# Two tiles' scores issued together in the first layer of a four-layer attention kernel, and its first chunk projected in blocks

## The chip, the cores and the metric

The kernel runs on one core of a Trainium2 chip. The metric is the time of the whole program on the device, in microseconds (us); the median of several executions counts. Engines are named as in the profile: PE (matmuls) and PEld (its weight loads), ACT (the scalar engine), DVE (the vector engine), POOL (GpSimd) and SP (the sync engine, which here issues most DMAs).

## The reference

Four layers in a row: A, B, A, B. Each normalises x, attends, projects and adds to x. A and B have weights of their own. The sequence is S = 2048, D = 640, 32 heads of 20. A attends in a causal window of 256 positions, B attends to all 2048 positions.

```python
def _A_ref(x, wqkv, wo):
    B, S, D = x.shape
    H = 32; Dh = D // H; W = 256
    qkv = (x @ wqkv).reshape(B, S, 3, H, Dh)          # shortened
    q, k, v = ...
    scores = jnp.einsum("bhqd,bhkd->bhqk", q, k) * (Dh ** -0.5)
    idx = jnp.arange(S)
    mask = (idx[:, None] - idx[None, :] >= 0) & (idx[:, None] - idx[None, :] < W)
    scores = jnp.where(mask[None, None], scores, -1e9)
    p = _softmax(scores, axis=-1)
    o = jnp.einsum("bhqk,bhkd->bhqd", p, v)
    return o.transpose(0, 2, 1, 3).reshape(B, S, D) @ wo
# _B_ref: the same without the mask
x = x + _A_ref(_layernorm(x), A_wqkv, A_wo)
x = x + _B_ref(_layernorm(x), B_wqkv, B_wo)
x = x + _A_ref(_layernorm(x), A_wqkv, A_wo)
x = x + _B_ref(_layernorm(x), B_wqkv, B_wo)
```

All tensors are bf16.

## The kernel before

**Units, sets and tiles.** The queries are worked on in four chunks of 512 (C = 512, c = 0 to 3), the heads in eight groups of four (g = 0 to 7). Layers are l = 0 to 3. A `Unit(l, c, g)` is the attention of one group for one chunk. It consists of sets: the scores of one head, one bank of PSUM, up to 512 columns. A windowed unit (layers 0 and 2) has 12 sets; those of the first chunk are partly narrower (512, 384 and 256 columns). Of the second layer's first chunk the units are cut into parts of four key blocks (16 sets each); 24 such early units are woven in among the first layer's later units, from (l, c, g) = (0, 1, 7) on. `index` numbers the units in their order: unit 16 is the first of the early ones, number 47 is (0, 3, 7), the last windowed unit of the first layer.

Sets are taken from the units in order into tiles. As long as units are narrow (the first layer and the early units), a tile has three sets when its number t is even and two when t is odd. Even tiles use banks 0 to 2 of PSUM, odd ones banks 3 and 4. Banks 5 and 6 serve the background work, bank 7 (`op`) sums the values.

**The main loop** (L1389 to L1559) does one tile per turn. It writes a fixed order of instructions:

1. the scores on PE (L1436: `lhsT` keys, `rhs` queries, 32 rows of the array each, up to four heads side by side);
2. one exp on ACT (L1462), or several where the widths differ, from PSUM into a tile `pt`;
3. background work (`background`, L1373), before the values while `state["early"]` holds and behind them otherwise;
4. the values: groups of four sets, at least three tiles old where the unit is windowed (L1495: 21 columns of the array for each head, summed in `op`);
5. the masks of the tile before: POOL (L1535) and DVE (L1546) zero parts of `pt`.

**Background work** is a list of tasks (`todo`) of Python generators, in the order of `need - lead`: `need` is the number of the unit that wants the result. `pump` lets tasks run for a credit per tile: 1.2 us up to unit 16, at most 1.0 after it. `require` runs tasks at once until something is ready. Tasks are the normalisation (`t_ln`), value projections (`t_v`), query and key projections in blocks of 128 rows (`t_block`), the output projection (`t_out`), and the tails of finished units, which divide by the sums. All of their matmuls go through `by_columns` (L311, shown as L315): four strips of 32 output columns side by side. Results leave PSUM through `evac`: on ACT (L345) up to unit 16, on DVE (L348) after it. `keep_clock` adds matmuls without a use (`masks,ident`) where a tile has little background.

**Queries and keys.** `t_block` casts a block of 128 rows to `st`, and POOL stores it to DRAM (`q_d`, `k_d`, L566). `load_unit` later loads a group's rows head by head from there into a slot of `qa` (4 slots) and of `ka` (18 slots), with eight DMAs on SP (L802, L803): 20 rows for each head at partitions 0, 32, 64 and 96. `load_ahead` starts the loads as soon as the blocks are ready and a slot is free. The first chunk of the first layer is different: `t_qk_first` projects each of the eight groups by itself, with weights padded from 20 to 32 columns a head (`get_w`: a memset on POOL and a copy on DVE), straight into `qa` and `ka`, without DRAM:

```python
        wt = take_w(0, g)
        q = qa_free.popleft()
        yield from project(wt, xnT[l, c], lambda: q[:])
        wt = take_w(1, g)
        k = ka_free.popleft()
        yield from project(wt, xnT[l, c], lambda: k[:])
```

`project` is five steps of four matmuls of 512 columns, and then `evac`.

**The beginning.** SP loads x's first chunk in two halves, then the first layer's query, key and value weights, the other chunks of x, and the second layer's value weights (L128 to L138). `first_ln` (L1254) normalises the first chunk; 14 matmuls without a use come first on PE (`warm(14)`, L1266), more stand between the transposes (L1284). `other_constants` zeroes `op` and builds the constants of the tails. `t_zeros` (L1232) zeroes `wop`, `kts` and `qts` by DMAs from zeroed `ka` slots, and loads the output weights (`load_wop`).

Of the kernel before, what the change touches and what calls it, by code (L numbers as in the profile page):

```python
# [18 lines left out]
P = 128  # L19
S = 2048  # L20
D = 640
# [24 lines left out]
KEEP = 30  # L46
HALF = True
# [10 lines left out]
def kernel(  # L58
# [77 lines left out]
    for c in range(1, NC):  # L136
        nc.sync.dma_start(out=x_sb[:, 4 * c : 4 * c + 4, :], in_=xin[:, 4 * c : 4 * c + 4, :])
    nc.sync.dma_start(out=wv_sb[1][:], in_=wq_view[1][:, :, 2 * D : 3 * D])  # L138
# [32 lines left out]

    nc.vector.memset(ka_all[:, G:KA, :], 0.0)

    def other_constants():
        nc.vector.memset(op, 0.0)
        nc.vector.tensor_copy(
            out=sel4[:], in_=ident[:].rearrange("p (j m) -> p j m", j=4)[:, :, DH]
        )

        nc.gpsimd.memset(spread8[:], 0.0)  # L180
        nc.gpsimd.memset(rts[:], 0.0)
        sp32 = rzp.tile([64, 2, 16], BF16, name="sp32", tag="sp32")
        sp16 = rzp.tile([64, 16], BF16, name="sp16", tag="sp16")
        for u in range(2):
            r = slice(32 * u, 32 * u + 32)
            nc.vector.tensor_copy(
                out=sp32[r], in_=ident[r, r].rearrange("p (n r) -> p n r", n=2)
            )
            nc.vector.tensor_tensor(
                out=sp16[r], in0=sp32[r, 0, :], in1=sp32[r, 1, :], op=ALU.add  # L190
            )
            nc.vector.tensor_copy(
                out=spread8[r, u].rearrange("p q (j m) -> p (q j) m", m=32),
                in_=sp16[r].unsqueeze(2).to_broadcast((32, 16, 32)),
            )
# [22 lines left out]
    def push(name, gen, need, left):  # L218
        lead = 0
        if type(name) is tuple and need <= first_use(1, NC - 1, 0):  # L220
# [3 lines left out]
            if name[0] in ("k", "q"):  # L224
                lead = 7 if name[1] == 1 and name[-1] == 0 else 2

            if name[0] == "stats" or name[:2] == ("ln", 0):
                lead = 5
# [82 lines left out]
    def by_columns(out_, lhsT, rhs, start, stop):  # L311

        for j in range(4):
# [39 lines left out]
    padded = [0]  # L353

    def get_w(n, i):

        a = padded[0] % 8 * P
        padded[0] += 1
        t = wqk[:, :, a : a + P]
        tv = t.rearrange("p c (j m) -> p c j m", j=4)  # L360
        nc.gpsimd.memset(tv[:, :, :, DH:32], 0.0)
# [18 lines left out]
    def block_w(l, n, b):  # L380

        a = n * D + b * P
# [13 lines left out]
    def project(wt, xt, dst):  # L396
# [6 lines left out]
        evac(dst(), pq)  # L403
# [17 lines left out]
    def t_ln(l, c):  # L421
# [3 lines left out]
        users[l, c] = 9 if (l, c) == (0, 0) else (11, 12, 11, 11)[l]  # L425
# [50 lines left out]
    def t_v(l, c, halves):  # L476
# [9 lines left out]
        for i in range(4):  # L486
            if windowed:
# [46 lines left out]
    ka_free = deque(kas)  # L534
    qa_free = deque(qas)

    def t_qk_first(l, c, g):
# [13 lines left out]
        if g == G - 1:  # L551
            nc.sync.dma_start(out=wqk[:], in_=wq_view[1][:, :, 0 : 8 * P])
            nc.sync.dma_start(out=wqk_rest, in_=wq_view[1][:, :, 8 * P : 2 * D])
            ready.add("weights")

    def t_block(l, n, c, b):
# [5 lines left out]
        wt = block_w(l, n, b)  # L562
        yield from project(wt, xnT[l, c], staged)
        rows = slice(b * P, (b + 1) * P)
        dst = k_d[l][rows, c * C : (c + 1) * C] if n else q_d[l][c, rows, :]
        nc.gpsimd.dma_start(out=dst, in_=staging.pop())  # L566
        used(l, c)
        ready.add(("qk"[n], l, c, b))
# [68 lines left out]
    def push_layer(l, c):  # L637
# [18 lines left out]
        for g in range(G):  # L656
            for n in (0, 1):
                worder[l, n].append((n, g))
            push(("qk", l, c, g), t_qk_first(l, c, g), need[g], 2.2)
            if g == 0:  # L660
                push(("v", l, c), t_v(l, c, (0, 1)), need[0], 5.6)
# [118 lines left out]
    small_units = deque(u for u in units if u.windowed and (u.l, u.c) != (0, 0))  # L780
# [45 lines left out]
    def unit_needs(u):  # L826
        l, c, g = u.l, u.c, u.g
        if (l, c) == (0, 0):
            return [("qk", l, c, g)]
# [27 lines left out]
    def start_unit(u):  # L857
        for n in unit_needs(u):
            require(n)
        if (u.l, u.c) != (0, 0):  # L860
# [371 lines left out]
    def t_zeros():  # L1232

        z = ka_all[:, G : G + 4, :].rearrange("p a b -> p (a b)")
        yield ("wait", 4)
# [6 lines left out]
        load_wop(0, False)  # L1242
        for t in (*kts, *qts):
# [10 lines left out]
    def first_ln():  # L1254

        users[0, 0] = 9
# [9 lines left out]
        warm(14)  # L1266
# [23 lines left out]
        for i in range(4):  # L1290
# [8 lines left out]
            if i > 0:  # L1299
                trs.append(scale(i - 1))  # L1300
                warm((0, 3, 2)[i - 1])
        nc.vector.tensor_copy(out=xt[:, :, 0:P], in_=trs[0])
        trs.append(scale(3))
        warm(3)
        nc.vector.tensor_copy(out=xt[:, :, P : 2 * P], in_=trs[1])
        for n in (1, 0):
            wtiles[n, 0] = get_w(n, 0)
        nc.vector.tensor_copy(out=xt[:, :, 2 * P : 3 * P], in_=trs[2])
        nc.scalar.copy(out=xt[:, :, 3 * P : 4 * P], in_=trs[3])
        mvs.pop((0, 0))  # L1310
# [3 lines left out]
    with tc.manual_schedule():  # L1314
# [4 lines left out]
        other_constants()  # L1319
# [60 lines left out]

        wide_pt = 0
        started = set()
        pts = deque()
        masked = None
# [3 lines left out]
        closed = -2  # L1388
        while ended is None or t < ended + 8:  # L1389
            t += 1  # L1390
            state["tick"] += 1
            n_b = 0
            if flow:
# [76 lines left out]
                if state["early"]:  # L1470
                    background(t, n_b)
# [4 lines left out]
            for n in range(2 if n_b == 0 or t > closed + 1 else 0):  # L1476
                u = pts[0][3][0] if pts else None
                size = 4
                if u is not None:
                    size -= sum(kc == pts[0][3][4][0][0] for kc, _ in u.aside)  # L1480
                if len(pts) < size or pts[size - 1][0] > t - n - (3 if u.windowed else 2):
                    break
                group = [pts.popleft() for _ in range(size)]
                subs, end = group[0][3][4], group[-1][3][7]
                if end and u.aside and pts and not side_ready(u) and group[-1][0] > t - 5:
                    pts.extendleft(reversed(group))
                    break
                first, last = group[0][3][5:7]
                if first and u.windowed:
                    require(("v", u.l, u.c, 0))  # L1490
                    require(("v", u.l, u.c, 1))
                for m, (kc, q0, qn, col) in enumerate(subs):
                    for _, pg, i, b in group:
                        j = b[1]
                        nc.tensor.matmul(  # L1495
                            op[32 * j : 32 * j + VW, q0 * P : (q0 + qn) * P],
                            lhsT=u.v(kc, j), rhs=pg[:, i, col * P : (col + qn) * P],
                            start=(first and m == 0), stop=not u.windowed or (last and m == len(subs) - 1),
                            skip_group_check=True,
                        )  # L1500
                if u.aside:
                    if end:
                        side_done(u)
                    else:
                        side_values(u, 3)
                if end:
                    pv_emitted(u)
                    finish_unit(u)
                    closed = t
                    break  # L1510

            if n_b and not freely():
                side_work(False, PRE_1)
            if n_b and not state["early"]:
                background(t, n_b)
            if n_b:
                side_work(False)
                columns = sum((4 - b[3]) * P for b in cur)
                state["lag"] = max(state["lag"] - columns / 1200 - 0.05, 0.0)

            if t > 0 and masked is not None:
                cur_, pt_ = masked
                i = 0
                while i < len(cur_):
                    m, b0 = cur_[i][2:4]
                    k = i
                    while k < len(cur_) and cur_[k][2] == m:
                        k += 1
                    split = m is not None
                    for b in ((3,), (1, 2), (0,))[m] if split else ():  # L1530
                        if b < b0:
                            continue
                        later = (m, b) in ((1, 1), (0, 3))
                        v = pt_[:, i:k, b * P : (b + 1) * P]
                        nc.gpsimd.affine_select(  # L1535
                            out=v, in_=v, compare_op=ALU.is_gt if later else ALU.is_ge, fill=0.0,
                            base=0, pattern=[[0, k - i], [-1 if later else 1, P]],
                            channel_multiplier=1 if later else -1,
                        )
                    if split and m != 1:  # L1540
                        cols = slice(max(b0, 0) * P, 2 * P) if m == 0 else slice(2 * P, C)
                        mv_ = masks[:, m, cols].unsqueeze(1).to_broadcast(
                            (P, k - i, cols.stop - cols.start)
                        )
                        state["lag"] += 0.45
                        nc.vector.tensor_tensor(  # L1546
                            out=pt_[:, i:k, cols], in0=pt_[:, i:k, cols], in1=mv_, op=ALU.mult
                        )
                    elif m is not None and not split:
                        cols = slice(max(b0, m == 1) * P, 3 * P if m == 1 else C)  # L1550
                        mv_ = masks[:, m, cols].unsqueeze(1).to_broadcast(
                            (P, k - i, cols.stop - cols.start)
                        )
                        state["lag"] += 0.45
                        nc.vector.tensor_tensor(
                            out=pt_[:, i:k, cols], in0=pt_[:, i:k, cols], in1=mv_, op=ALU.mult
                        )
                    i = k
            masked = (cur, pt) if n_b else None  # L1559
# [35 lines left out]
```

## Time and profile before

| what | us |
|---|---|
| median of 3 runs (lowest to highest) | 2161.81 (2161.41 to 2163.21) |
| the profiled execution's own time | 2161.74 |
| its span, first to last instruction | 2160.0 |
| PE busy | 1926.8 (89%) |
| ACT busy | 2088.0 (97%) |
| DVE busy | 1467.3 (68%) |
| POOL busy | 361.5 (17%) |
| exps (L1462), 1641 of them | 2054.0 |

The span is one execution, seen by the hardware profiler; 1.7 us of its own time lie outside of it. Busy time of PE counts a matmul from its start to its modelled end, so matmuls that follow each other closely overlap, and a busy PE need not be at its peak. A row of a timeline gives the start and the length of merged instructions, engine, line, operation, what is written from what, shapes (rows of the array by columns, then elements), the count, and in brackets how long the engine stood idle before it and for what.

### The profile page before, as it was taken

The numbers are of one execution on the slowest core, as the hardware profiler recorded it, in microseconds if no ns is written. First come the engines' busy times: TensorE is split into PE (matmuls) and PEld (weight loads), VectorE is DVE, ScalarE is ACT, GpSimd is POOL, SyncE is SP. The second block draws the span as 40 slices with busy tenths as digits, with TensorE's granted clock in tenths as the row PEclk, the third lists the DMA queues.
The fourth block names the chain that finished last, engine by engine and source line by source line (L and its number), as shares of the span: only waits on it lengthen the run. The fifth ranks groups of instructions, "written<-read, shape, count | busy, mean of one in ns | idle before, by whom it ended". The sixth has DMA issues, their size and how long they took to land. (4 is left out here: it accounts for less than half of the span.)

```text
span 2160.0 us, 73146 instructions
## 1 busy us (share of the span) xinstructions
PE 1926.8 (89%) x31790; PEld 757.8 (35%) x31791; DVE 1467.3 (68%) x2613; ACT 2088.0 (97%) x1717; POOL 361.5 (17%) x805
## 2 busy tenths in 40 slices
PE   8899999988889898888988989888898988888898
PEld 4444443433333333333333433342332222222222
DVE  6556665426666776776767743773588888987886
ACT  7889899999999999999999999999999999999997
POOL 6543434000022002400033001500000000000000
PEclk9999999999999999999999999999999999999999
DMA  6212122222110222111120122111111111111100
GB/s 204 65 54 75 54 62 69 67 63 59 55 42 27 63 53 69 38 31 48 50 83 27 33 60 75 33 45 52 54 57 44 36 36 42 32 33 39 44 27 17
DMA packets 81440, 114.33 MB, mean 53 GB/s; under 512 B 20990, under 2 KB 63070, under 8 KB 81118
## 3 DMA queue, kind: packets, MB, share of 16 engines
q1 hardware_dynamic: 71502, 81.06, 14.2%
q0 software_dynamic: 9616, 28.59, 3.8%
q8 instruction: 249, 4.08, 0.8%
q14 instruction: 73, 0.60, 0.1%
HBM read 76.58 MB, written 27.79 MB: 48 GB/s over the span
## 5 line engine op out<-in xcount | busy, mean ns | idle before, releaser
L1462 ACT ACTIVATE pt<-ps 128x1536 bf16<-128x1536 f32 (+2 forms) x1641 | 2054.0, 1417 | 38.5 <-PE ps L1436 28.9
L1436 PE MATMUL ps<-qt,kt 32*128 32x512 bf16 x3913 | 543.6, 384 | 62.8 <-ACT pt L1462 55.7
L315 PE MATMUL ps<-masks,ident 128*32 128x512 bf16 x5684 | 507.6, 384 | 94.7 <-ACT pt L1462 49.1
L1495 PE MATMUL ps<-pt,vt 128*21 128x512 bf16 x3784 | 377.1, 386 | 0.3 <-ACT pt L1462 0.2
L1436 PEld LDWEIGHTS <-kt 32*128 32x128 bf16 x3913 | 155.5, 91 | 460.1 <-issue 440.8
L315 PEld LDWEIGHTS <-ident 128*32 128x32 bf16 x5684 | 182.2, 94 | 283.4 <-issue 256.7
L1535 POOL TENSOR_SCALAR_AFFINE_SELECT pt<-pt 128x256 bf16<-128x256 bf16 (+2 forms) x508 | 219.0, 453 | 198.6 <-ACT pt L1462 185.8
L348 DVE CAST st<-ps 128x512 bf16<-128x512 f32 x134 | 92.6, 691 | 144.8 <-PE ps L315 144.5
L1495 PEld LDWEIGHTS <-vt 128*21 128x21 bf16 x3784 | 93.7, 89 | 254.2 <-issue 250.5
L315 PE MATMUL ps<-wop,on 128*32 128x320 bf16 x3712 | 160.7, 300 | 4.5 <-DVE x_sb L598 2.6
L1007 DVE TENSOR_SCALAR spare<-ps 128x512 int32<-128x512 f32 x200 | 137.2, 686 | 27.8 <-PE ps L989 24.1
L315 PEld LDWEIGHTS <-on 128*32 128x32 bf16 x5760 | 122.8, 95 | 62.3 <-issue 28.4
L1546 DVE TENSOR_TENSOR pt<-pt,masks 128x256 bf16<-128x256 bf16 (+3 forms) x270 | 117.0, 449 | 39.5 <-ACT pt L1462 37.6
L1436 PE MATMUL ps<-qa,ka 32*128 32x384 bf16 (+2 forms) x1408 | 118.5, 275 | 22.9 <-ACT pt L1462 19.6
L1203 DVE TENSOR_TENSOR on<-on,ps 128x512 bf16<-128x512 bf16 x128 | 86.4, 684 | 59.0 <-PE ps L315 56.9
L598 DVE TENSOR_TENSOR x_sb<-x_sb,ps 128x320 bf16<-128x320 bf16 x120 | 58.3, 486 | 100.3 <-PE ps L315 99.5
L315 PE MATMUL ps<-wv,xnT 128*32 128x320 bf16 x2560 | 117.1, 303 | 9.5 <-DVE on L1203 3.0
L315 PE MATMUL ps<-xnT,spare 128*32 128x512 bf16 x1720 | 118.0, 381 | 5.5 <-DVE on L1203 1.8
L315 PE MATMUL ps<-xnT,wqk 128*32 128x512 bf16 x1600 | 107.7, 381 | 4.6 <-DVE rts L1182 1.3
L1007 DVE TENSOR_SCALAR raw_o<-ps 128x512 int32<-128x512 f32 x112 | 76.8, 686 | 47.6 <-PE ps L1436 46.7
L900 DVE CAST on<-ps 128x512 bf16<-128x512 f32 x112 | 76.7, 685 | 35.5 <-PE ps L1495 28.5
L566 POOL DMA_DIRECT2D k_d<-st x75 | 41.6, 555 | 270.9 <-DVE st L348 248.0
(103 smaller groups left out, 1731.6 us busy)
## 6 DMA issues: line engine op xcount, KB each, us to landing
vt<-v_d SPq DMA_DIRECT2D x48, 336.0 KB
kt<-k_d SPq DMA_DIRECT2D x192, 80.0 KB
k_d<-st POOLq DMA_DIRECT2D x75, 128.0 KB, 2.2
q_d<-st POOLq DMA_DIRECT2D x75, 128.0 KB, 2.1
qt<-q_d SPq DMA_DIRECT2D x384, 20.0 KB
v_d<-vs POOLq DMA_DIRECT2D x16, 336.0 KB, 3.0
qa<-q_d SPq DMA_DIRECT2D x224, 20.0 KB
ka<-k_d SPq DMA_DIRECT2D x224, 20.0 KB
```

Of the source, the lines that this page charges most:

```text
L315: nc.tensor.matmul(out_[r], lhsT=lhsT[:, r], rhs=rhs, start=start, stop=stop)
L348: nc.vector.tensor_copy(out=out_, in_=in_)
L566: nc.gpsimd.dma_start(out=dst, in_=staging.pop())
L598: nc.vector.tensor_tensor(out=xv, in0=had, in1=yp, op=ALU.add)
L900: nc.vector.tensor_copy(out=oT, in_=op)
L1007: nc.vector.tensor_scalar(out=xi.bitcast(I32)[:, i * C : (i + 1) * C], in0=z, scalar1=SCALE * LOG2E * FIX, scalar2=127.5 * FIX, op0=ALU.mu ...
L1203: nc.vector.tensor_tensor(out=oT, in0=oT, in1=zb, op=ALU.mult)
L1436: nc.tensor.matmul(sp[:, i, col * P : (col + qn) * P], lhsT=u.k(kc, j), rhs=u.q(j, q0, qn), start=True, stop=True,)
L1462: nc.scalar.activation(out=pt[:, i:k, b0 * P :], in_=sp[:, i:k, b0 * P :], func=ACT.Exp, scale=SCALE,)
L1495: nc.tensor.matmul(op[32 * j : 32 * j + VW, q0 * P : (q0 + qn) * P], lhsT=u.v(kc, j), rhs=pg[:, i, col * P : (col + qn) * P], start=(first ...
L1535: nc.gpsimd.affine_select(out=v, in_=v, compare_op=ALU.is_gt if later else ALU.is_ge, fill=0.0, base=0, pattern=[[0, k - i], [-1 if later ...
L1546: nc.vector.tensor_tensor(out=pt_[:, i:k, cols], in0=pt_[:, i:k, cols], in1=mv_, op=ALU.mult)
```

## The change

It has three parts.

- **Pairs.** While the running unit is before (0, 3, 7) (`paired()`), an even tile's scores and exps are followed at once by the next tile's scores and exps. Only then come the even tile's background, values and masks, and after these the odd tile's (`rest`, the former steps 3 to 5, otherwise unchanged but for the `require` of the values).
- **First chunk in blocks.** Only groups 0 and 1 are projected by `t_qk_first`. The rows of the other six groups, 160 to 640, become four blocks (`FIRST`), projected by `t_block` and passed through DRAM like the other chunks. The value projection is split in two halves of the heads, and a unit requires only its own half.
- **Beginning.** Fewer warm-up matmuls come first and a little more later (9, then 2, 3, 3 and 4, instead of 14, then 0, 3, 2 and 3). Two weight tiles and two `qa` slots are zeroed at the start. The tails' constants, chunks 2 and 3 of x, and the second layer's value weights move into `t_zeros`. The zero rows of six more `ka` slots come by DMA. The second layer's query and key weights are loaded after the last block (`load_b`). Some leads change.

```diff
+FIRST = ((160, 288), (288, 416), (416, 544), (544, 640))
...
-    for c in range(1, NC):
+    def load_x(c):
         nc.sync.dma_start(out=x_sb[:, 4 * c : 4 * c + 4, :], in_=xin[:, 4 * c : 4 * c + 4, :])
-    nc.sync.dma_start(out=wv_sb[1][:], in_=wq_view[1][:, :, 2 * D : 3 * D])
+    load_x(1)
...
+    for n in range(2):
+        nc.gpsimd.memset(
+            wqk[:, :, n * P : (n + 1) * P].rearrange("p c (j m) -> p c j m", j=4)[:, :, :, DH:32], 0.0
+        )
     nc.vector.memset(ka_all[:, G:KA, :], 0.0)
-    def other_constants():
-        nc.vector.memset(op, 0.0)
+    nc.vector.memset(qa_all[:, 2:QA, :], 0.0)
+    def end_constants():
...
-                lead = 7 if name[1] == 1 and name[-1] == 0 else 2
+                lead = 7 if name[1] == 1 and name[-1] == 0 else 1 if name[1:] == (0, 0, 2) else 2
...
-                lead = 5
+                lead = 12 if name[0] == "stats" else 5
...
-        for j in range(4):
+        for j in range(lhsT.shape[-1] // 32):
...
-    ka_free = deque(kas)
+    ka_free = deque(kas[0:2] + kas[G + 4 : KA] + kas[2 : G + 4])
...
-        wt = block_w(l, n, b)
+        wt = block_w(l, n, c, b)
         yield from project(wt, xnT[l, c], staged)
-        rows = slice(b * P, (b + 1) * P)
+        rows = slice(*FIRST[b]) if (l, c) == (0, 0) else slice(b * P, (b + 1) * P)
         dst = k_d[l][rows, c * C : (c + 1) * C] if n else q_d[l][c, rows, :]
-        nc.gpsimd.dma_start(out=dst, in_=staging.pop())
+        nc.gpsimd.dma_start(out=dst, in_=staging.pop()[0 : rows.stop - rows.start])
         used(l, c)
+        if (l, n, c, b) == (0, 0, 0, len(FIRST) - 1):
+            load_b()
...
-        for g in range(G):
+        for g in range(2):
             for n in (0, 1):
                 worder[l, n].append((n, g))
-            push(("qk", l, c, g), t_qk_first(l, c, g), need[g], 2.2)
+            push(("qk", l, c, g), t_qk_first(l, c, g), 0, 2.2)
             if g == 0:
-                push(("v", l, c), t_v(l, c, (0, 1)), need[0], 5.6)
+                for n in (1, 0):
+                    push(("qk"[n], l, c, 0), t_block(l, n, c, 0), 2, 1.1)
+                push(("v", l, c, 0), t_v(l, c, (0,)), 0, 2.8)
+        for b, g in enumerate((2, 3, 5, 6)):
+            if b == 0:
+                continue
+            if b == 2:
+                push(("v", l, c, 1), t_v(l, c, (1,)), 4, 2.8)
+            for n in (1, 0):
+                push(("qk"[n], l, c, b), t_block(l, n, c, b), g, 1.1)
...
-        yield ("wait", 4)
+        yield ("wait", 3)
+        end_constants()
+        for n in (2, 5):
+            nc.gpsimd.dma_start(
+                out=ka_all[:, n : n + 3, :].rearrange("p a b -> p (a b)"), in_=z[:, 0 : 3 * C]
+            )
+        yield ("wait", 1)
+        load_x(2)
...
         load_wop(0, False)
+        yield ("wait", 8)
+        load_x(3)
+        nc.sync.dma_start(out=wv_sb[1][:], in_=wq_view[1][:, :, 2 * D : 3 * D])
+        yield ("wait", 3)
...
-        warm(14)
+        warm(9)
...
-                warm((0, 3, 2)[i - 1])
+                warm((2, 3, 3)[i - 1])
+        wtiles[0, 0] = get_w(0, 0)
         nc.vector.tensor_copy(out=xt[:, :, 0:P], in_=trs[0])
         trs.append(scale(3))
-        warm(3)
+        warm(4)
         nc.vector.tensor_copy(out=xt[:, :, P : 2 * P], in_=trs[1])
-        for n in (1, 0):
-            wtiles[n, 0] = get_w(n, 0)
         nc.vector.tensor_copy(out=xt[:, :, 2 * P : 3 * P], in_=trs[2])
         nc.scalar.copy(out=xt[:, :, 3 * P : 4 * P], in_=trs[3])
+        wtiles[1, 0] = get_w(1, 0)
...
+        def rest(t, n_b, cur, pt):
+            nonlocal closed, masked
+            if n_b and state["early"]:
+                background(t, n_b)
+            for n in range(2 if n_b == 0 or t > closed + 1 else 0):
...
+                if first and u.windowed:
+                    require(("v", u.l, u.c, u.g // 4))
...
+            masked = (cur, pt) if n_b else None
+
+        def paired():
+            return state["unit"] < index[0, 3, 7, None] and len(flow) > 0
...
             t += 1
-            state["tick"] += 1
+            state["tick"] += behind is None
...
+            if n_b and t % 2 == 0 and paired():
+                behind = (t, n_b, cur, pt)
+                continue
+            if behind is not None:
+                rest(*behind)
+                state["tick"] += 1
+                behind = None
+            rest(t, n_b, cur, pt)
```

## The prediction

> **What bounds the kernel now.** I read the page first: ScalarE (ACT) is busy for 97% of the span. Then I cut the span into stages with the table of windows, since an average over stages hides where ACT is idle. Columns: stretch, length, busy time (instructions) of PE, PEld, DVE, ACT, POOL, then granted clock and DMA.
>
> ```profile
> 0.00:16.00 16.00, 11.38 (x82) 4.85 (x82) 12.25 (x34) 6.48 (x8) 9.93 (x33) 1.00 0.93 284
> 16.00:52.00 36.00, 33.20 (x673) 16.04 (x677) 20.95 (x60) 30.48 (x52) 22.32 (x54) 1.00 0.52 160
> 52.00:130.00 78.00, 68.95 (x1705) 36.28 (x1698) 47.38 (x127) 64.67 (x86) 39.02 (x94) 0.98 0.20 63
> 130.00:200.00 70.00, 65.38 (x1330) 30.20 (x1329) 38.77 (x78) 65.78 (x66) 32.34 (x76) 1.00 0.28 82
> 200.00:300.00 100.00, 92.72 (x1919) 43.26 (x1914) 63.39 (x136) 89.19 (x77) 37.28 (x88) 0.97 0.21 59
> 300.00:366.00 66.00, 63.18 (x1294) 28.50 (x1293) 42.83 (x94) 63.87 (x56) 28.22 (x64) 1.00 0.22 64
> 366.00:2160.00 1794.00, 1591.94 (x24803) 598.62 (x24802) 1241.72 (x2087) 1767.51 (x1378) 192.40 (x398) 1.00 0.17 46
> ```
>
> From 366 us on ACT is busy for 1767.5 of 1794 us, and the change touches nothing there: what is saved before it goes through to the end one for one. Before 366, where the first layer's units lie, ACT is idle for 9.5 us up to its first exp, then for 5.5, 13.3, 4.2, 10.8 and 2.1 us (length minus ACT busy), 36 us in all. The waits of ACT from 16 to 366 us say for what:
>
> ```profile
> ACT pt L1462 <- PE ps L1436: 17.9, 33, 1.6
> ACT st L345 <- PE ps L315: 4.3, 7, 1.4
> ACT ka L345 <- PE ps L315: 2.8, 5, 1.2
> ACT va L345 <- PE ps L315: 1.9, 4, 1.0
> ACT qa L345 <- PE ps L315: 1.5, 3, 0.7
> ```
>
> The exps (L1462) wait for the scores (L1436), and ACT's own evacuation casts (L345) wait for the projections (L315): PE is late, and it is busy for 92 to 96% of these windows. So I looked at PE's timeline, instruction by instruction:
>
> ```profile
> 253.97 0.39 PE L1436 MATMUL ps<-qt,kt 32*128 32x512 bf16 x3
> 254.29 0.86 PE L315 MATMUL ps<-wv,xnT 128*32 128x320 bf16 x20
> 255.09 0.39 PE L1436 MATMUL ps<-qt,kt 32*128 32x512 bf16 x2
> 255.41 0.86 PE L315 MATMUL ps<-wv,xnT 128*32 128x320 bf16 x20
> 256.10 0.39 PE L1495 MATMUL ps<-pt,vt 128*21 128x512 bf16 x4
> 256.42 0.39 PE L1436 MATMUL ps<-qt,kt 32*128 32x512 bf16 x3
> 258.07 1.26 PE L315 MATMUL ps<-xnT,spare 128*32 128x512 bf16 x20
> ```
>
> Scores use strips of 32 rows, everything else strips of 32 columns. From scores to the background is 0.32 us (253.97 to 254.29), from values back to scores 0.32 us (256.10 to 256.42). Inside one form 20 matmuls, four at a time, take 1.26 us, so a step of 512 columns is (1.26 - 0.39) / 4 = 0.22 us. A change of form therefore costs 0.10 us, twice in every tile. Last, ACT's timeline:
>
> ```profile
> 165.63 34.98 ACT L1462 ACTIVATE pt<-ps 128x1536 bf16<-128x1536 f32 x30 [1.55 <-PE ps L1436]
> ...
> 254.49 4.78 ACT L1462 ACTIVATE pt<-ps 128x1536 bf16<-128x1536 f32 x4 [0.34 <-PE ps L1436]
> ```
>
> Undelayed, 30 exps (three and two banks in turn) take 34.98 us: 2.33 us a pair. And a late exp starts 0.52 us after its score (253.97 to 254.49).
>
> **How many pairs.** By the code the paired stretch holds 31 windowed units of 12 sets and 16 early units of 16: 628 sets, 2.5 a tile, 251 tiles, some 126 pairs. The first 16 units (192 sets, 38 pairs) run while ACT also evacuates, up to about 148 us, where its last cast stands; the other 87 pairs take the 218 us up to 366, that is 2.5 us each against ACT's 2.33.
>
> **Part 1, the start.** The first chain is x, statistics, scaling on ACT, transposes, projection, score, exp at 16.73 us. The first normalised tile ends at about 7.5 us (ACT row at 6.55, two in 1.98), but 14 warm-up matmuls hold PE from 3.65 to 9.57 us (5.92, 0.42 each), and the transposes start at 9.41. Nine end at about 7.4. That frees up to 1.8 us there; ACT's third scaling (waiting 1.40 us for these transposes) follows, but DVE's copies and the added wqk copy ahead of them (1.97 us for two) then lead the chain, so I take -0.7 (0 to -1.5). The added `qa` memset on DVE (a fifth of the 2.19 us of `ka`'s by size is 0.4) fits in DVE's 0.65 us wait for x, and two wqk memsets on POOL (0.25 each) in POOL's 0.78 us idle; without these covers they cost 0.4 and 0.5. The constants moved behind the first tiles put 0.95 + 0.42 us of memsets on POOL among the masks; values are taken three tiles after their exp, over 3 us, so nothing waits. x chunks 2 and 3 and the second layer's value weights move down SP's queue behind the first-layer weights; chunk 1 is wanted first and stays early.
>
> **Part 2, the first chunk in blocks.** Before: 8 groups, q and k, 16 projections. After: 4 for the first two groups and 8 of blocks, 12. (The last block, 96 rows, has 15 matmuls but the same five steps.) Four projections less are 4 x 5 x 0.22 = 4.4 us of PE and 4 x 0.59 = 2.4 us of ACT casts (`ka`, `qa` mean 0.59). From 16 to 52 us PE is busy for 92%, ACT for 85% and partly for just these casts, so most of it is on the path: -4, between -2.4 (ACT's part alone) and -6 (with the value projections of the second half, 4 x 0.86 us, no longer ahead of the second unit). New cost: groups 2 to 7 go through DRAM, 8 block stores on POOL (0.56 us each) and 48 loads on SP; hidden if they lead by enough, see the rivals. The loads also stand behind `load_wop` on SP, which in the trace of before took 39.79 to 42.11 us waiting for its zeros.
>
> **Part 3, the pairs.** Two changes of form of four go: 0.20 us of PE a pair. Let W be the background and values of a pair. PE needs 2 x (0.32 + 0.10) + W = W + 0.84 before and 0.22 + 0.32 + 0.10 + W = W + 0.64 after. But the second score of a pair writes the banks that the exp just ahead reads, so PE now stands at it until ACT ends the last odd exp, with both tiles' background and values queued behind; and the next even exp waits for a score behind those. From that end: some 0.1 to the score (an estimate; the rows don't split it), 0.32, W, 0.10, 0.52 to the exp, W + 1.04, and the exps in between cover 2.33. Over that circle of two pairs a pair takes at least (W + 3.37) / 2. So before is max(2.33, W + 0.84), after max(2.33, W + 0.64, (W + 3.37) / 2): they cross at W = 1.69, at 2.53 us a pair. Slower pairs gain, up to 0.20; pairs in which ACT now runs undelayed lose, at most 0.10 (W = 1.49).
>
> In the first 38 pairs (16 to 148 us, 132 / 38 = 3.5 us a pair) PE decides: the full gain is 38 x 0.20 = 7.6, and casts that wait for their projection, 10.5 us in the lines shown, then find two exps ahead of them. Some of ACT's idle time there waits for DVE or for work that a unit's start demands at once, which pairs don't touch: -6 (-2 to -12). In the 87 later pairs the mean, 2.5, lies at the crossing, but unevenly: at 165 to 200 us ACT isn't idle, at 218 to 260 it is every second tile. The ends are +9 (87 x 0.10) and -15 (all of the (2.5 - 2.33) x 87); idle comes in bursts of W over 2, so -3.
>
> **The sum**, against the profiled execution, 2161.74 us (span 2160.0; median of the runs 2161.81): -0.7 - 4 - 6 - 3 = -13.7, 2148.
>
> [...] The granted clock is 0.91 in 80 to 100 us and 0.94 in 200 to 220, with PE busy for 15.5 and 17.6 of 20 us and no wait of PE over 1.3 us in either; 20 x 0.09 = 1.8 us of clock for one such drop. Pairs gather PE's pauses in one place, so drops could double: three more are 5 us of PE.
> [...]
>
> **Rivals.** (a) *The circle takes the gain.* The late pairs cost their +9 and the early ones bring -2: -0.7 - 4 - 2 + 9 = +2, about 2160 to 2164. For it: ACT undelayed from 165 to 200 us. Against: 10.8 us idle between 200 and 300. 16%. (b) *The way through DRAM makes it slower.* A block's cast at 57.52 us leads to stores at 58.40 and 59.81, landing 2.1 us later, loads from 61.93, eight in some 3 us, and again a landing: 8 us. If units 2 to 7 lead by half of that, each waits 4 us, 24 in all: 2148 + 24 = 2172. It decides once a block's cast is less than 8 us ahead of its unit. Against: each block is queued two or more units ahead, and a unit takes 36 / 8 = 4.5 us. 11%. (c) *PE sheds nearly all of its lateness*, ACT idle only for some 10 us in the stretch: 36 + 2.4 - 10 = 28 less, 2133. 8%.
>
> **Numbers.** My forecast, faster by 5 to 24 us, has 65%. The range takes it in with part of (a) above and part of (c) below: 2133 to 2163; (b) is left out. About 0.2%, 4.3 us, is what a measurement can tell. Faster by more: 65 + 8 + 3 of (a), 76%; within: 11% (of (a)); slower: 11 + 2, 13%.
>
> **What would show it.** Right: the first exp near 16.0; 12 projections before the second chunk's normalisation, and that earlier by 4 us or more; score bursts of five matmuls at 0.22 us; ACT's wait for L1436 below 12 us; the unchanged stretch still about 1794 us long. Wrong: PE waiting long for a DMA of `qa` or `ka` before 60 us (b); PE's wait for ACT growing from 6.6 us (110 to 380 us) with ACT idle after every second exp at 165 to 200 us (a).

## The result, and the profile after

The change made the kernel slower: 2176.85 us median of 6 runs (2175.16 to 2179.89) against 2161.61 us (2159.39 to 2163.21), a ratio of 1.0073 with a 95% interval of [1.0062, 1.0084]. The forecast was 2148 us, in 2133 to 2163. The profiled execution took 2175.78 us, its span 2173.8 us.

The windows of the changed kernel, cut like those of before but for the end (line numbers have moved: the scores are L1575 instead of L1436, the exps L1601 instead of L1462, `by_columns` is L321, ACT's casts L351, the values L1451, POOL's masks L1491):

```profile
0.00:16.00 16.00, 11.51 (x98) 4.78 (x102) 10.74 (x29) 7.18 (x9) 8.03 (x28) 1.00 0.80 236
16.00:52.00 36.00, 28.66 (x627) 15.28 (x623) 17.02 (x46) 27.64 (x49) 20.62 (x45) 1.00 0.43 135
52.00:130.00 78.00, 64.64 (x1634) 39.92 (x1630) 44.28 (x113) 58.93 (x86) 41.60 (x101) 0.96 0.38 117
130.00:200.00 70.00, 58.86 (x1353) 31.00 (x1347) 37.29 (x87) 61.69 (x63) 30.01 (x70) 1.00 0.27 79
200.00:300.00 100.00, 86.97 (x1864) 43.15 (x1857) 59.21 (x134) 90.78 (x79) 38.10 (x90) 1.00 0.21 60
300.00:366.00 66.00, 59.53 (x1200) 27.98 (x1198) 39.99 (x88) 61.49 (x53) 28.79 (x64) 0.97 0.23 65
366.00:380.00 14.00, 11.45 (x227) 4.80 (x224) 5.50 (x13) 14.00 (x14) 3.74 (x8) 1.00 0.11 29
380.00:2173.00 1793.00, 1590.93 (x24801) 598.16 (x24798) 1241.12 (x2086) 1767.10 (x1377) 192.24 (x397) 1.00 0.17 46
```

From 380 us on everything is as it was: 1793 us with 1767.1 us of ACT, where before 1794 had 1767.5. All of the loss lies in the first layer's stretch. ACT's idle time there (length minus busy) is 8.4, 19.1, 8.3, 9.2, 4.5 and 0 us from 16 to 380 us, 49.5 us against 36.0 before. And PE, which was to become the freer engine, is busy for only 80 to 90% of these windows where it had been for 88 to 96: now both engines stand idle in turn. What PE waits for from 16 to 148 us (in total, times, longest):

```profile
PE ps L321 <- ACT st L351: 6.4, 7, 1.4
PE ps L321 <- ACT xnT L351: 4.7, 4, 2.1
PE ps L321 <- ACT vs L351: 3.5, 2, 1.8
PE ps L321 <- DVE on L1235: 2.9, 3, 1.9
PE ps L1451 <- DVE nmr L447: 2.7, 1, 2.7
...
PE ps L321 <- ACT va L351: 1.7, 1, 1.7
```

PE's background waits 16.3 us for ACT's casts (6.4 + 4.7 + 3.5 + 1.7); before the change these four kinds came to 4.8 us:

```profile
PE ps L315 <- ACT xnT L345: 2.6, 5, 1.2
PE ps L315 <- ACT st L345: 0.8, 3, 0.3
PE ps L315 <- ACT va L345: 0.7, 2, 0.5
PE ps L315 <- ACT vs L345: 0.7, 1, 0.7
```

ACT's timeline, and below it PE's, show how such a wait comes about (start, length, ..., idle time ahead and its cause):

```profile
42.55 0.59 ACT L351 CAST st<-ps 128x512 bf16<-128x512 f32 x1 [0.76 <-PE ps L321]
43.04 2.41 ACT L1601 ACTIVATE pt<-ps 128x256 bf16<-128x256 f32 x3
45.34 0.58 ACT L351 CAST st<-ps 128x512 bf16<-128x512 f32 x1
47.27 0.58 ACT L351 CAST st<-ps 96x512 bf16<-96x512 f32 x1 [1.35 <-PE ps L321]
```

```profile
42.87 1.26 PE L321 MATMUL ps<-xnT,spare 128*32 128x512 bf16 x20
43.95 0.39 PE L1451 MATMUL ps<-pt,va 128*21 128x384 bf16 x8
44.17 0.43 PE L321 MATMUL ps<-sel,on 128*32 128x4 bf16 x32
45.97 0.83 PE L321 MATMUL ps<-xnT,spare 128*32 128x512 bf16 x9 [1.37 <-ACT st L351]
```

The even tile's projection is finished at 44.13 us. Its cast stands on ACT behind both tiles' exps (43.04 to 45.45) and frees its bank at 45.92. A tail has taken the other background bank at 44.17, so the odd tile's projection waits for the first one's: PE idle for 1.37 us. Then ACT has only that projection's cast next and is idle for 1.35 us. Here each engine waits for the other once; in the changed kernel's four rows of waits PE waits so 14 times (7 + 4 + 2 + 1) in some 38 pairs.

The sign that the prediction named for its rival (a) came in part: PE's wait for ACT's exps from 110 to 380 us grew from 6.6 to 19.1 us. ACT's wait for the scores, which was to fall below 12 us, is 16.9 us from 16 to 380 us. The sign for rival (b) didn't come: before 60 us PE doesn't wait for a DMA of `qa` or `ka`.

### The profile page after: what moved, and what is told of

Read it like the earlier page. It is cut to its first block, busy times and chain, and to the rows that moved or that the text cites. A ratio compares the mean times of both kernels' runs of the same rounds, so it can differ in the third digit from the quotient of the medians.

```text
span 2173.8 us, 73183 instructions
## 1 busy us (share of the span) xinstructions
PE 1912.6 (88%) x31767; PEld 765.1 (35%) x31768; DVE 1455.2 (67%) x2592; ACT 2088.8 (96%) x1723; POOL 363.1 (17%) x803
## 5 line engine op out<-in xcount | busy, mean ns | idle before, releaser
L1601 ACT ACTIVATE pt<-ps 128x1536 bf16<-128x1536 f32 (+2 forms) x1641 | 2049.8, 1415 | 43.9 <-PE ps L1575 27.6
L1575 PE MATMUL ps<-qt,kt 32*128 32x512 bf16 x3913 | 542.2, 383 | 72.4 <-ACT pt L1601 64.7
L321 PE MATMUL ps<-masks,ident 128*32 128x512 bf16 x5752 | 512.6, 384 | 97.0 <-ACT pt L1601 49.6
L1451 PE MATMUL ps<-pt,vt 128*21 128x512 bf16 x3784 | 376.6, 386 | 0.3 <-ACT pt L1601 0.2
L1575 PEld LDWEIGHTS <-kt 32*128 32x128 bf16 x3913 | 154.5, 91 | 468.9 <-issue 448.3
L321 PEld LDWEIGHTS <-ident 128*32 128x32 bf16 x5752 | 184.2, 94 | 286.8 <-issue 259.4
L1491 POOL TENSOR_SCALAR_AFFINE_SELECT pt<-pt 128x256 bf16<-128x256 bf16 (+2 forms) x508 | 218.0, 453 | 201.2 <-ACT pt L1601 192.5
L1451 PEld LDWEIGHTS <-vt 128*21 128x21 bf16 x3784 | 94.0, 89 | 252.6 <-issue 248.7
L354 DVE CAST st<-ps 128x512 bf16<-128x512 f32 x126 | 87.1, 691 | 137.9 <-PE ps L321 137.7
L321 PE MATMUL ps<-wop,on 128*32 128x320 bf16 x3712 | 160.5, 300 | 5.6 <-DVE x_sb L615 3.0
L321 PEld LDWEIGHTS <-on 128*32 128x32 bf16 x5760 | 125.0, 95 | 60.3 <-issue 25.4
L1575 PE MATMUL ps<-qa,ka 32*128 32x256 bf16 (+2 forms) x1408 | 112.0, 275 | 28.7 <-ACT pt L1601 24.0
L321 PE MATMUL ps<-xnT,spare 128*32 128x512 bf16 x1870 | 127.4, 380 | 10.5 <-ACT st L351 3.8
L321 PE MATMUL ps<-wv,xnT 128*32 128x320 bf16 x2560 | 115.3, 302 | 9.9 <-DVE va L354 1.9
L321 PE MATMUL ps<-xnT,wqk 128*32 128x512 bf16 x1360 | 92.3, 380 | 4.0 <-ACT st L351 1.4
```

What stands on the lines that cost most here:

```text
L321: nc.tensor.matmul(out_[r], lhsT=lhsT[:, r], rhs=rhs, start=start, stop=stop)
L354: nc.vector.tensor_copy(out=out_, in_=in_)
L1451: nc.tensor.matmul(op[32 * j : 32 * j + VW, q0 * P : (q0 + qn) * P], lhsT=u.v(kc, j), rhs=pg[:, i, col * P : (col + qn) * P], start=(first ...
L1491: nc.gpsimd.affine_select(out=v, in_=v, compare_op=ALU.is_gt if later else ALU.is_ge, fill=0.0, base=0, pattern=[[0, k - i], [-1 if later ...
L1575: nc.tensor.matmul(sp[:, i, col * P : (col + qn) * P], lhsT=u.k(kc, j), rhs=u.q(j, q0, qn), start=True, stop=True,)
L1601: nc.scalar.activation(out=pt[:, i:k, b0 * P :], in_=sp[:, i:k, b0 * P :], func=ACT.Exp, scale=SCALE,)
```

## The experiments

Two theories were tried first: "banks", the mechanism just shown, and its rival that the way through DRAM and the moved beginning cost the time. Ratios are against the kernel before, measured beside each run, with their 95% intervals. Most intervals reach some 2 us either way, so a difference between two runs of under some 3 us isn't clear of noise.

**Without pairs.** `paired()` returns False; blocks and beginning stay.

```diff
-            return state["unit"] < index[0, 3, 7, None] and len(flow) > 0
+            return False
```

> The changed kernel without the pairs: blocks and reordered beginning alone. Theory 'banks' (in a pair the two exps stand ahead of ACT's evacuation casts, so the two banks of background come free only after both exps, and PE and ACT wait for each other in turn): the loss goes, and start (-1) and four projections less (-4) remain, less some 2 us for the constants on POOL: 2156 to 2161 us. Theory 'DRAM and beginning' (the first chunk's way through DRAM and the moved constants, loads and statistics cost the time, the pairs are harmless): still slow, 2172 to 2177 us.

Measured: 2160.66 us, 0.9996 [0.9987, 1.0005]. The pairs are the whole loss, 16 us; blocks and beginning together come out even.

**Pairs alone**, put into the kernel before (its main loop replaced by the changed one).

> The kernel before with the pairs alone, first chunk and beginning as before. Theory 'banks': slower than before by 8 to 14 us, 2170 to 2176 us, and PE's wait for ACT's casts before 148 us grows from 6 us to over 12. Theory 'DRAM and beginning': pairs save changes of form on PE, so 2150 to 2161 us.

Measured: 2175.6 us, 1.0065 [1.0052, 1.0079]. The same loss without any of the other parts. PE's wait for ACT's casts before 148 us, all kinds together, is 12.0 us, where the kernel before had 6.2. The rival theory falls.

**Pairs only from unit 16 on**, where DVE evacuates.

```diff
+            return woven <= state["unit"] < index[0, 3, 7, None] and len(flow) > 0
```

> The changed kernel with pairs only from unit 16 on, where DVE evacuates and ACT runs exps alone. Theory 'banks': no loss there, since no cast stands behind an exp: within 4 us of the run without any pairs, 2154 to 2162 us. Theory 'DRAM and beginning': 2172 to 2177 us. A third, 'circle' (PE stands at the second score until the last exp ends): slower than without pairs by 5 to 9 us.

Measured: 2169.52 us, 1.0034 [1.0021, 1.0046]: 8.9 us slower than without pairs. So "banks" is only half of it (2176.85 - 2169.52 = 7.3 us are the early pairs'), and "circle" is the other half, at the upper end of what it expected. ACT's exps from 148 to 372 us, forms apart (count, busy, mean ns, idle time before and its causes), without pairs and then with late pairs:

```profile
L1601 ACT ACTIVATE pt<-ps 128x1536 bf16<-128x1536 f32 x93 | 137.2, 1475 | 6.2 <-PE ps L1575 4.1 <-POOL pt L1491 0.8 <-POOL rstd L441 0.4
L1601 ACT ACTIVATE pt<-ps 128x1024 bf16<-128x1024 f32 x93 | 97.3, 1047 | 1.6 <-PE ps L1575 1.3
```

```profile
L1601 ACT ACTIVATE pt<-ps 128x1536 bf16<-128x1536 f32 x89 | 129.8, 1458 | 17.2 <-PE ps L1575 10.5 <-issue 4.2 <-POOL pt L1491 1.4
L1601 ACT ACTIVATE pt<-ps 128x1024 bf16<-128x1024 f32 x89 | 91.9, 1033 | 0.0
```

All idle time now stands ahead of the three-bank exps, the first of a pair, and none ahead of the second: 17.2 us against 7.8 (6.2 + 1.6), so 9.4 us more, which is the loss. (Of the 17.2 the profile puts 4.2 down to no cause.) PE's wait at the scores for an exp in the same stretch, without pairs and then with late pairs:

```profile
PE ps L1575 <- ACT pt L1601: 7.1, 24, 0.5
```

```profile
PE ps L1575 <- ACT pt L1601: 19.2, 47, 0.6
```

Taken wait by wait, 39 of the 47 (16.5 us) are for the two-bank exp of an odd tile; without pairs 9 were (2.9 us). One circle in the run with late pairs, on PE:

```profile
239.96 0.39 PE L1575 MATMUL ps<-qa,ka 32*128 32x384 bf16 x4 [0.30 <-ACT pt L1601]
240.28 1.54 PE L321 MATMUL ps<-wv,xnT 128*32 128x320 bf16 x40
241.65 0.39 PE L1451 MATMUL ps<-pt,va 128*21 128x128 bf16 x8
241.97 0.63 PE L1575 MATMUL ps<-qt,kt 32*128 32x512 bf16 x5
```

and on ACT:

```profile
237.54 4.62 ACT L1601 ACTIVATE pt<-ps 128x1536 bf16<-128x1536 f32 x4 [0.52 <-PE ps L1575]
242.52 7.00 ACT L1601 ACTIVATE pt<-ps 128x1536 bf16<-128x1536 f32 x6 [0.36 <-PE ps L1575]
```

PE has stood for 0.30 us at the second score until 239.96. Background and values of both tiles follow, the next score at 241.97, its exp at 242.52, 2.56 us after the second score began, while the two exps in between give ACT 2.33 us of work: 0.36 us idle before it.

**The even tile's cast between the two exps.** In a pair, `background` of the even tile is called ahead of the odd tile's exp. PE's order stays.

```diff
-            if n_b and state["early"]:
+            if n_b and state["early"] and t not in done_b:
                 background(t, n_b)
...
+                if behind is not None and state["early"]:
+                    done_b.add(behind[0])
+                    background(behind[0], behind[1])
                 i = 0
```

> The changed kernel; in a pair the even tile's background is issued ahead of the odd tile's exp, so that PE's order is the same and on ACT the even tile's casts come between the two exps, as before the change. Theory 'banks': a bank comes free one exp (1.0 us) earlier, PE's wait for ACT's casts before 148 us falls from 16 us to about 6 to 9, and the time to 2162 to 2168 us. Theory 'DRAM and beginning': unchanged within 2 us, 2175 to 2179 us.

Measured: 2168.89 us, 1.0031 [1.002, 1.0043], 8.0 us faster than the changed kernel. PE's wait of the background for casts before 148 us, the sum above, falls from 16.3 to 6.3 us:

```profile
PE ps L321 <- ACT xnT L351: 2.3, 3, 1.2
PE ps L321 <- ACT st L351: 1.6, 4, 0.6
PE ps L321 <- ACT vs L351: 1.6, 2, 0.9
PE ps L321 <- ACT va L351: 0.8, 1, 0.8
```

Its wait at the scores for exps grows, from 1.7 to 4.6 us, and the time is 0.9 us above the range expected. "Banks" is shown for the early pairs: only ACT's order was changed.

**The even tile's values between the scores**, late pairs only: `values(t, n_b)` is called for the even tile before the odd tile's scores, instead of in `rest`.

> As the run with pairs only from unit 16 on, but the even tile's values are issued between the two tiles' scores: as many changes of form on PE as without pairs, and less work between the second score and the next pair's first. Theory 'circle' (ACT's last odd exp ends, PE's second score, the background and values of both tiles, the next even score, its exp): the values taken out of the circle, some 0.25 us a pair, halved over two pairs, 87 pairs: about 10 us, so the 9 us that the late pairs cost go almost wholly: 2160 to 2164 us. Theory 'changes of form' (the saved changes are the gain and something else costs 9 us): 8 to 17 us worse, 2177 to 2186 us.

Measured: 2166.52 us, 1.0025 [1.0015, 1.0034]: 3.0 us better than late pairs, a third of what was expected and within the noise, and not worse as the rival expected. PE's waits at the scores for an exp fall from 19.2 to 10.1 us (from 148 to 372 us). That speaks for the circle; but this order also gives back the saved changes of form, and the two are not separated here.

**One set in odd tiles, without and with late pairs.** Odd tiles from unit 16 on have one set, in banks 3 and 4 in turn, so a second score no longer writes what the last odd exp reads.

```diff
-                size = 2 if t % 2 and narrow(flow[0]) else 3
+                size = (1 if late_units() else 2) if t % 2 and narrow(flow[0]) else 3
...
+                if n_b == 1 and t % 4 == 3:
+                    sp = ps[:, 4:7, :]
```

> A base for the next run: no pairs, and from unit 16 to (0, 3, 7) odd tiles have one set instead of two, in banks 3 and 4 in turn. The 436 sets there make 109 pairs of four sets instead of 87 of five, so 22 more of both tile and exp, each with a fixed part of some 0.15 to 0.2 us on ACT and 0.20 us of changes of form on PE: 3 to 12 us slower than without pairs, 2164 to 2173 us. Both theories agree here.

> The same with pairs from unit 16 on. The second score now writes a bank that was read two odd exps ago, so PE doesn't stand at it until ACT ends the last odd exp. Theory 'circle': the pairs' loss of 9 us goes, and the saved changes of form (up to 0.20 us for each of 109 pairs) are left where PE is late: equal to or faster than the run before it, by 0 to 15 us. Rival 'two tiles of background in one piece' (the late pairs cost because background and values of two tiles come in one stretch, whatever banks the scores use): again slower than the run before it, by 5 to 12 us.

Measured: 2192.83 us without pairs (1.0143 [1.0129, 1.0157]; the base was expected to take at most 2173 us) and 2179.89 us with them (1.0083 [1.007, 1.0097]). With the banks apart the same pairs gain 12.9 us where they had lost 8.9. ACT's wait for scores from 150 to 390 us, first without pairs, then with:

```profile
ACT pt L1607 <- PE ps L1581: 13.6, 29, 1.4
```

```profile
ACT pt L1607 <- PE ps L1581: 6.7, 13, 1.0
```

So the saved changes of form can reach the end (12.9 us over 109 pairs would be 0.12 us a pair, if all of the gain is theirs), and two tiles' background in one piece doesn't by itself make pairs slow. PE still waits for exps here, 30.9 us against 13.2 without pairs, but in 71 of 72 waits for a three-bank exp of an even tile, and never for the one-bank exp of an odd one: the second score's wait is gone. One thing is not separated: PE was later in this base than in the run without pairs above (its exps waited 13.6 us for scores, there 5.4 us from 148 to 372 us), so there was also more for pairs to save.

**Pairs only before unit 16, with the cast between the exps.**

> The changed kernel with pairs only before unit 16, and ACT's cast of the even tile between the two exps. Theory 'banks': the early pairs cost 7 us for the order of the casts alone, and with this order they are harmless or gain a little from fewer changes of form: 2156 to 2162 us, as without pairs (2160.7). If the early pairs have a price beyond it: 2164 to 2168 us.

Measured: 2156.82 us, 0.9982 [0.9973, 0.9991], 3.8 us faster than without pairs, just clear of noise. Where PE is the late engine, pairs gain once the casts are in the right order. The gain doesn't simply add to the rest: with the late pairs in place the same early pairs bring only 0.6 us (2168.89 against 2169.52).

**Constants back at the start**, without pairs: `end_constants()` is called before the first exp instead of in `t_zeros`.

> The changed kernel without pairs, and the tails' constants built ahead of the first exp again instead of behind the first tiles. In the run without pairs POOL's two memsets and the moved copies stand ahead of masks, and PE waits 1.7 us for them. Theory 'moved constants' cost that: 1 to 3 us faster than without pairs, 2158 to 2160 us. Rival 'given back': a gain before unit 16 is only time in which background is done earlier or later, and the end doesn't move: 2160 to 2161.5 us.

Measured: 2158.98 us, 0.9988 [0.998, 0.9997], 1.7 us faster than without pairs, as expected, but within the noise. The wait itself is seen in the traces: 2.7 us in the changed kernel, 1.7 us without pairs (`PE ps L1451 <- DVE nmr L447` both times), and it is gone with the constants at the start. POOL's timeline of the changed kernel shows the place:

```profile
31.95 0.94 POOL L186 MEMSET spread<- 128x1024 bf16 x1
32.84 0.45 POOL L187 MEMSET rts<- 128x384 bf16 x1
33.24 1.33 POOL L1270 DMA_DIRECT2D ka<-ka  x2
34.65 0.20 POOL L441 TENSOR_SCALAR rstd<-mv 128x4 f32<-128x4 f32 x1
34.93 1.04 POOL L444 TENSOR_TENSOR rstd<-rstd,nhalf 128x4 f32<-128x4 f32 x1
35.95 0.40 POOL L1491 TENSOR_SCALAR_AFFINE_SELECT pt<-pt 128x256 bf16<-128x256 bf16 x1
```

Four microseconds of memsets, issuing of zero DMAs and the second chunk's statistics stand ahead of one mask; its values start on PE at 36.40 us:

```profile
36.40 0.34 PE L1451 MATMUL ps<-pt,va 128*21 128x384 bf16 x2 [2.70 <-DVE nmr L447]
```

This is the 2.7 of the waits above. The profile names DVE's `nmr`, which ended at 36.37 us; but the values read `pt`, and the mask that writes it ended at 36.35.

**The first chain alone**, in the kernel before: 9 warm-up matmuls first, the weight tiles' order and memsets.

> The kernel before with the first chain alone changed: fewer warm-up matmuls at first, the weight tiles' order and their memsets. First exp at 15.5 instead of 16.7 us. If the start goes through to the end: 2160 to 2160.7 us; if it is taken back behind it: 2161.4 us, no difference.

Measured: 2161.46 us, 1.000 [0.9991, 1.0009]. The first exp starts at 15.6 instead of 16.7 us, but the gain isn't seen at the end; the interval of 2 us either way can't tell 0.7 us from nothing.

**What paid, together**: blocks and beginning, constants at the start, pairs before unit 16 with the cast between; then the same with the statistics' lead back at 5.

> The parts that paid, together: blocks and beginning, constants built ahead of the first exp, pairs only before unit 16 with the cast between the exps. If the gains add (-4.5 and -1.7 against the kernel before): 2153 to 2156 us. If they are the same idle time saved twice: 2156 to 2158 us.

> As the run before it, but the statistics of the later chunks keep their old lead of 5 units instead of 12, so that the second chunk's normalisation isn't brought ahead of the first chunk's blocks. Theory 'order': the exps 12 to 60, 7 us longer than in the kernel before, get shorter by 3 to 7 us, and 1 to 4 us of it reach the end: 2150 to 2155 us. Rival 'given back': the second chunk's work has to be done anyway, so the end is the same within 1 us or later.

Measured: 2154.71 us, 0.9971 [0.996, 0.9982], the fastest of all and faster than both kernels: the gains nearly add. With the old lead 2159.84 us, 0.9994 [0.9986, 1.0003], so the theory "order" is wrong about the end: with the lead of 12 the second chunk's normalisation does make the stretch from exp 12 to exp 60 longer (62.8 us against 58.6, by the exps' starts in the two traces), but the 200 exps after it take 258.9 us instead of 269.9. Why is not settled, since the granted clock differs too: from 148 to 250 us it is 1.00 with the lead of 12 and 0.97 with 5, its mean over an execution has the medians 0.998 and 0.996, and at the same mean of 0.997 the two kernels' times don't differ (one execution with 2157.79 us against two with 2156.28 and 2159.03).

## Why the prediction was wrong, step by step

**The bound and the pass-through** were right: nothing after the first layer's stretch moved, and what was lost in it reached the end. (PE was busy for 88 to 96% of the windows from 16 us on, not for 92 to 96%: the stretch from 52 to 130 us has 68.95 of 78 us.)

**Part 3, early pairs (-6, bounds -2 to -12): wrong, +7.3.** The step that failed is the sentence that casts "then find two exps ahead of them". That was counted as a gain for ACT. It was not followed to the next user of the bank: a cast behind two exps holds one of only two background banks, and a third use in the pair waits for it (PE for 1.37 us until 45.97 us). With the cast between the exps, and no late pairs, the early ones gain: -3.8, half of the bound of 7.6.

**Part 3, late pairs (-3, bounds +9 to -15): the mechanism was right, its size mis-chosen.** The circle, W + 1.04 against 2.33 us, was worked out before the run and the row of 239.96 us follows it. (The 0.1 us in it from an exp's end to the score was the author's estimate; the trace of before shows 0.05 us, an exp of 1.45 us from 182.01 us and the score it held up at 183.51.) It was weighed as a rival and costs 8.9 us net, as much as its full bound (87 x 0.10). Two things were missed. The ACT idle time that stood for -15 was taken from the kernel before; but the other parts had already taken half of it: without pairs the exps' idle time from 148 to 372 us is 7.8 us (6.2 + 1.6), so there was little left to gain. And the later pairs were held to gain on balance, while PE stood at a score for an odd tile's exp 39 times, which without pairs it had done 9 times.

**Part 2 (-4) and part 1 (-0.7): together with the moved constants -0.8, within the noise.** Without the constants' delay it is -2.4 (2158.98 against 2161.34), where -4.7 was forecast; the start by itself showed no gain at the end. Twelve projections ran for sixteen, and the first exp came at 15.65 us. But only eight of the twelve stood before the second chunk's normalisation, which the longer lead of the statistics brought from 49.55 to 36.40 us; the last four have their casts from 42.55 us on. How much of the missing gain that explains no run shows. The claim "so nothing waits" for the constants was wrong, by 2.7 us of PE's wait: the masks' three tiles of slack were eaten because POOL also had zero DMAs (1.33 us) and the second chunk's statistics (0.20 and 1.04 us) in the queue ahead of them.

**The moved lead of the statistics** was named nowhere in the sum. In the kernel with the parts that paid it goes with 5 us (2159.84 - 2154.71). Background brought forward loads the early stretch, where ACT is idle anyway, and may relieve the later one; that the clock made part of the difference, or all of it, is not ruled out.

**Rival (b), the way through DRAM**, came nearest in time (2172) for a wrong reason: the blocks and the beginning, without pairs, cost nothing together. Rival (a), the circle, was the mechanism of half the loss, but was priced without the banks.

**The clock.** In the two profiled executions it fell alike: its mean over the span is 0.997 with the change, 0.998 before. Over all executions that isn't so: the mean is 0.995 to 0.997 in the six of the changed kernel (median 0.996), and 0.996 to 0.999 in the eleven without pairs (median 0.998). The kernel before took 2160.3 us (median) in its executions at 0.998 and 2162.1 us in those at 0.996. By that, some 2 of the 16 us may be the clock's (an estimate), so the 5 us that the prediction set against the pairs were too many, but perhaps not without ground; no run separates them. That pauses of PE bring the drops was the author's guess, and no run shows it: in the kernel before the clock is 0.94 from 280 to 300 us with PE busy for 19.39 of 20 us, and 1.00 from 40 to 60 us with 17.15. The clock isn't the main cause, since the order of the casts alone gives back 8.0 us and the late pairs alone cost 8.9.

## What to carry to other kernels

When instructions are regrouped on one engine, follow each buffer to its next user: a release that moves behind a longer instruction can cost more than the regrouping saves (the casts' order alone gave back 8.0 us here). Where two engines hand buffers back and forth with two copies only, pairing the work on one of them can close a circle (the late pairs lost 8.9 us here); work out its period and compare it with each engine's own, stage by stage, using the idle time that is left after the change's other parts. Test an order of instructions by changing one engine's order alone, as the cast between the exps does here.

## What the runs showed of the hardware

A change of form between strips of rows and strips of columns on PE costs 0.10 us here: 0.32 us from one to the other (253.97 to 254.29 and 256.10 to 256.42 us before, 239.96 to 240.28 and 241.65 to 241.97 us with late pairs) against 0.22 us for a step within one form (238.26 to 238.48 us with late pairs, values to background). Saved twice a pair, at most 0.12 us of the 0.20 reached the end, in the run with the banks apart (12.9 us over 109 pairs).
